# Second channel product by one level of Strassen's method, token groups of 512, and a new order

## The chip, the cores and the metric

The kernel runs on one core of one Trainium2 chip. The metric is the device time of one execution in microseconds (us), a median of runs. The engines are PE (matmul), with its weight loads PEld beside it, DVE (vector), ACT (scalar), POOL (GpSimd) and SP, which issues the DMAs. Each engine works its own queue in order; a semaphore wait at the head of a queue holds all that stands behind it.

## The reference, cut to what matters

Three layers in a row, on 2 samples x 768 tokens x 384 channels, all in fp32:

```python
y[t]  = rt @ (state + u * outer(kt, vt))           # layer 1: attention, per head of 48,
state = wt[..., None] * state + outer(kt, vt)      #          over 768 steps
h = gelu(x @ w_in); u, v = h[..., :512], h[..., 512:]
x = x + (u * (w_sg @ (norm(v) * g) + b_sg)) @ w_out        # layer 2: gated MLP
u  = x + (relu(x.T @ w_tok1) @ w_tok2).T           # layer 3: mixer, 768 -> 256 -> 768
return u + relu(u @ w_ch1) @ w_ch2                 #          and 384 -> 1536 -> 384
```

## The kernel before, in words

Every fp32 operand of a large product is held as two parts, hi (a copy rounded to the matmul's fp32r type) and lo (the rest). `prod` makes a product from three matmuls into one PSUM tile: hi.hi (L257), hi.lo (L258), lo.hi (L259).

The weights arrive as 64-bit floats and are converted on the chip in chunks, in three stages (`advance`): stage 0 two ACT instructions (L214, L215), stage 1 two on DVE (L217, L219), stage 2 a hi copy on ACT (L224) and the lo subtraction on POOL (L226; on DVE for the early weights). A chunk waits in one of four buffers named st; a freed buffer is loaded again by a DMA that SP issues.

The order of all work before the channel stage is written by hand in two strings, ORDER (attention and the first product of layer 2) and LAST (the rest of layer 2, token products, staging). Each letter calls one part: 0, 1, 2 advance one chunk by that stage; w is one keep-warm matmul (L125); P and Y are the attention's outputs (L608; L617 and L623), Q its state sum (L641, L647), i and j the first token product and its eviction (T1p, T1e), k and l the second (T2p, T2e), m one C1 of token group 0. p frees the transposed inputs and opens the last pools. L617 and L647 add a vector that DVE has made, or the old state, into the PSUM sum, by a matmul with the identity.

The mixer's channel stage works on four groups of 384 tokens. `C1(h, j)` makes hidden tile j (of 12) of group h: nine matmuls of 384 columns, then `relu_split`: ACT writes hi (L398), DVE lo (L399). `C2(h, j, ct)` adds hidden tile j into the output tile ct (of 3): three matmuls of 384. The first C1 group stands in LAST (m); `rest()` then alternates C1(h+1, j) and the three C2(h, j, ct), and at the end C2 of group 3, one ct after the other, each with one DVE add (L454) and one store (L455).

PSUM has eight banks; in the channel stage five turn for C1 and three hold the sums of C2.

## Time and profile before

| | us |
|---|---|
| median of 3 runs (lowest, highest) | 390.64 (390.48, 390.92) |
| the profiled execution | 391.98 |
| its span, first to last instruction | 390.3 |
| PE busy | 379.9 (97%) |
| DVE busy | 233.5 (60%) |
| ACT busy | 187.8 (48%) |
| POOL busy | 133.1 (34%) |

The rows that follow below come from this profiled execution. A row of the time line gives the start of an instruction, its duration, engine, line, operation, the tile written and those read, and a count; matmuls overlap, so what one costs is the distance from its start to the next one's. In brackets stands the idle time ahead, with its releaser.

### The profile page before, as it was taken

How to read it: one execution, taken by the hardware profiler on the slowest of the kernel's cores; microseconds unless marked ns; L12 is line 12 of the kernel's file. 1: busy time of each engine (PE TensorE's matmuls, PEld its weight loads, DVE VectorE, ACT ScalarE, POOL GpSimd, SP SyncE). 2: the span in 40 equal slices, each digit the busy share in tenths (PEclk: the TensorE clock that was granted, in tenths of full speed). 3: DMA queues.
4: the chain of work that ended last, by engine and by line, in shares of the span. 5: the costliest groups of instructions: out<-in, count | busy, mean ns of one | idle time of the engine just before them, and what ended most of it. 6: DMA issues, size and time to landing. Idle time of an engine off the chain costs nothing.

```text
span 390.3 us, 7950 instructions
## 1 busy us (share of the span) xinstructions
PE 379.9 (97%) x3229; PEld 354.8 (91%) x3229; DVE 233.5 (60%) x396; ACT 187.8 (48%) x427; POOL 133.1 (34%) x149
## 2 busy tenths in 40 slices
PE   8899999999999999999999999999999999999994
PEld 3487788889999799999999999999999999999993
DVE  7999998889797575794486674782133114211320
ACT  3699878887345795754546674741111111111000
POOL 2325577763543356567544651350000000000000
PEclk9999999999999999999999999999999999999998
DMA  7575375453361014322433242400010001000110
GB/s 238 172 215 181 100 246 155 122 156 114 94 214 42 2 40 123 107 66 71 123 102 102 81 126 78 121 3 0 3 44 18 1 0 62 0 2 0 64 40 27
DMA packets 15581, 33.68 MB, mean 86 GB/s; under 512 B 2352, under 2 KB 5680, under 8 KB 15536
## 3 DMA queue, kind: packets, MB, share of 16 engines
q1 hardware_dynamic: 15536, 33.09, 27.9%
q8 instruction: 27, 0.44, 0.5%
q14 instruction: 18, 0.15, 0.1%
HBM read 30.72 MB, written 2.36 MB: 85 GB/s over the span
## 4 chain that ended last, share of the span: by engine, by line
PE 83%; POOL 4%; ACT 3%; issue 3%; DVE 3%; DMA 2%; SPq 1%; POOLq 0%; ACTq 0%
PE mm L257 23%; PE mm L258 23%; PE mm L259 23%; PE py L623 3%; PE pa L582 2%; PE py L608 2%; DMA st<-in_dram 1%; PE tr L282 1%; POOL vs L367 1%; PE pkv L641 1%; DMA kr<-in_dram 1%; PE mm L567 1%; PE mm L420 1%; PE py L617 1%; PE pt L595 1%
## 5 line engine op out<-in xcount | busy, mean ns | idle before, releaser
L399 DVE SCALAR_TENSOR_TENSOR cl<-mm,ch 128x384 fp32r<-128x384 f32 x48 | 26.5, 556 | 83.9 <-ACT ch L398 83.9
L398 ACT ACTIVATE ch<-mm 128x384 fp32r<-128x384 f32 x48 | 23.4, 492 | 93.1 <-PE mm L259 93.0
L217 DVE SCALAR_TENSOR_TENSOR st<-st 128x384 int32<-128x384 int32 (+1 forms) x50 | 30.3, 607 | 9.5 <-ACT st L215 7.9
L219 DVE SCALAR_TENSOR_TENSOR st<-st 128x384 int32<-128x384 int32 (+1 forms) x50 | 33.2, 665 | 1.7
L214 ACT ACTIVATE st<-st 128x384 f32<-128x384 f32 (+1 forms) x50 | 25.8, 517 | 9.3 <-DMA st<-in_dram 9.3
L588 POOL TENSOR_SCALAR_AFFINE_SELECT A<-A 128x512 f32<-128x512 f32 x24 | 18.3, 770 | 33.5 <-ACT A L587 32.0
L215 ACT ACTIVATE st<-st 128x384 int32<-128x384 uint32 (+1 forms) x50 | 25.5, 510 | 0.0
L369 ACT ACTIVATE gh<-vs 128x384 fp32r<-128x384 f32 x16 | 8.4, 524 | 32.9 <-POOL vs L367 32.9
L367 POOL TENSOR_TENSOR vs<-vs,uT 128x384 f32<-128x384 f32 x16 | 19.2, 1205 | 11.6 <-DVE vs L365 11.6
L560 POOL TENSOR_TENSOR rk<-kr 112x512 f32<-112x512 f32 x12 | 19.0, 1580 | 11.4 <-DMA kr<-in_dram 11.4
L257 PE MATMUL mm<-xt,wuh 128*128 128x256 f32 x72 | 20.8, 289 | 0.0
L259 PE MATMUL mm<-xt,wul 128*128 128x256 f32 x72 | 20.3, 282 | 0.0
L258 PE MATMUL mm<-xt,wuh 128*128 128x256 f32 x72 | 20.3, 282 | 0.0
L534 DVE TENSOR_TENSOR_SCAN wf<-wf,scan 112x516 f32<-112x516 f32 x12 | 19.0, 1583 | 1.6 <-DMA wf<-in_dram 1.6
L548 DVE TENSOR_TENSOR_SCAN wf<-wf,scan 112x516 f32<-112x516 f32 x12 | 17.8, 1480 | 0.4
L391 POOL TENSOR_TENSOR x1l<-x,x1h 128x384 fp32r<-128x384 f32 x12 | 14.0, 1173 | 10.4 <-ACT x1h L390 10.4
L125 PE MATMUL mm<-scan 112*128 112x512 bf16 x49 | 14.2, 431 | 3.1 <-DVE scan L673 1.7
L556 DVE TENSOR_TENSOR kr<-kr,wf 112x1024 f32<-112x1024 f32 x12 | 15.9, 1328 | 1.2 <-DVE wf L548 0.2
L257 PE MATMUL mm<-ch,c20h 128*128 128x384 f32 x48 | 16.1, 336 | 0.2 <-DVE o L454 0.2
L257 PE MATMUL mm<-woh,gh 128*128 128x384 f32 x48 | 16.2, 338 | 0.0
L259 PE MATMUL mm<-woh,gl 128*128 128x384 f32 x48 | 16.1, 336 | 0.0
L257 PE MATMUL mm<-uh,c10h 128*128 128x384 f32 x48 | 16.1, 336 | 0.0
(188 smaller groups left out, 1233.3 us busy)
## 6 DMA issues: line engine op xcount, KB each, us to landing
st<-in_dram SPq DMA_DIRECT2D x38, 384.0 KB, 3.4
kr<-in_dram SPq DMA_DIRECT2D x12, 448.0 KB, 4.3
st<-in_dram SPq DMA_DIRECT2D x18, 256.0 KB, 4.2
...
ub<-in_dram SPq DMA_DIRECT2D x1, 3.5 KB, 4.6
```

The costliest lines, as they stand in the source:

```text
L214: nc.scalar.activation(high.bitcast(F32), high.bitcast(F32), AF.Copy, scale=REBIAS)
L215: nc.scalar.activation(low, low.bitcast(U32), AF.Copy, scale=TOP3, bias=FLOOR)
L217: nc.vector.scalar_tensor_tensor(low, high, -2 ** 31, low, op0=ALU.bitwise_and, op1=ALU.bitwise_or)
L219: nc.vector.scalar_tensor_tensor(low, high, 3, low, op0=ALU.logical_shift_left, op1=ALU.bitwise_or)
L257: mm(out, w[0], x[0], start=first, stop=False, skip_group_check=True)
L258: mm(out, w[0], x[1], start=False, stop=False, skip_group_check=True)
L259: mm(out, w[1], x[0], start=False, stop=last, skip_group_check=True)
L367: nc.gpsimd.tensor_tensor(t, t, self.uT[d, h], op=ALU.mult)
L398: nc.scalar.activation(hi, ps, AF.Relu)
L399: nc.vector.scalar_tensor_tensor(lo, ps, 0.0, hi.bitcast(F32), op0=ALU.max, op1=ALU.subtract)
L534: nc.vector.tensor_tensor_scan(WF[i][:, WCOL + 2:], WF[i][:, :NHP * CW], scan1.rearrange("p h c -> p (h c)"), 0.0, op0=ALU.mult, op1=ALU.add)
L560: nc.gpsimd.tensor_tensor(RK[i][:PR], KR[i][:, 0], KR[i][:, 1], op=ALU.mult)
```

## The change

The channel stage now takes three groups of 512 tokens. C1(g, k) makes hidden tiles 2k and 2k+1, each by nine matmuls of 512 columns. For the pair of hidden tiles (b1, b2), each split in two halves of 256 tokens, and the first two output tiles, C2(g, k) forms the 2 x 2 block product by seven block products of 256 columns instead of eight (Winograd's form of Strassen's method), three matmuls each; the third output tile is done directly by four (C2d). So a step has 33 matmuls of 256 in C2 and 18 of 512 in C1, and there are 18 steps.

The method needs sums on both sides. Sums of weight blocks are made once, on POOL (`sums_of_weights`) and ACT with POOL (`split_sums`), for k = 0 before the first step and for each next k beside it. Sums of activations (ta, tb) are made in the eviction of C1, which is now eight DVE and six ACT instructions a step. At the end of a group `finish` combines the seven products with the residual (which POOL makes in steps 1 to 3 of each group) in eight DVE adds, one ACT copy and three POOL adds, `finish_rest` in two more DVE adds, and six stores of 256 tokens go out. Of the last group, 24 direct matmuls of k = 4 and 5 stand after the last Strassen product.

T2 follows the groups: its parts are 512, 256, 256, 512 tokens wide per output tile (EDGES). The identity matmuls L617 and L647 are issued in two column halves, 64 wide. C1 no longer stands in LAST. Both strings are new; keep-warm matmuls are 49 as before. Pools moved, and C1 turns three PSUM banks, C2 five.

```diff
@@ -25,6 +25,9 @@
 EPS = 1e-6
 NHP = H // 2
 PR = 112
+G = 2 * P
+EDGES = 0, 4, 6, 8, 12
+BPAD = 112
@@ -55,14 +58,14 @@
 ORDER = (
-    "w0010w 1www1w w201Tw wwtwqL FSQwUw wZwAge ww0wwo Kw0Nw1 20F2ww ww1qw2 2wTYyt SoXxe2 PUQA0Z KgVYL0 qyS1XN T10eAF "
+    "w00q10 T11t2w ww0QZg 10wwww wU0FwS wANwwK wwwqwe wNowww Lw1202 T1Y22F StUAyX PoxQ2Z eKg0V0 LY11Sy qXeT0N AoFUB0 "
...
 LAST = (
...
-    "2mij1j 0mlmkk k01lkk 1k22l0 l20ll0 11210m 1222l")
+    "01122i 0lkjjk klk200 11l2k1 kl01ll 2kll22")
...
@@ -407,7 +411,7 @@
             self.prod(ps, self.wp("t1", k, c, DTOK), self.x1[b * NC + k], k == 0, k == NC - 1)
     def T1e(self, n):
-        hi, lo = self.a2(F32R, E, "hh"), self.a2(F32R, E, "hl")
+        hi, lo = self.a15(F32R, "hh"), self.a15(F32R, "hl")
         self.relu_split(self.tps.pop(n), hi, lo)
         self.tok[n] = hi, lo
@@ -415,44 +419,154 @@
         nc, (h, ct) = self.nc, divmod(n, 3)
         c = slice(ct * P, (ct + 1) * P)
-        ps = self.ups[n] = self.mm(E)
-        for j in range(3):
-            nc.tensor.matmul(ps[:, j * P:(j + 1) * P], self.x[3 * h + j][:, c], self.ident,
-                             is_transpose=True, start=(j == 0), stop=False, skip_group_check=True)
+        n0, n1 = EDGES[h:h + 2]
+        ps = self.ups[n] = self.mm((n1 - n0) * P)
+        for j in range(n0, n1):
+            nc.tensor.matmul(ps[:, (j - n0) * P:(j - n0 + 1) * P], self.x[j][:, c], self.ident,
+                             is_transpose=True, start=(j == n0), stop=False, skip_group_check=True)
         for j in range(2):
             self.prod(ps, [t[:, c] for t in self.tok[h // 2 * 2 + j]],
-                      self.wp("t2", j, slice(h % 2 * E, (h % 2 + 1) * E), S), False, j == 1)
+                      self.wp("t2", j, slice((n0 - h // 2 * NC) * P, (n1 - h // 2 * NC) * P), S), False, j == 1)
     def T2e(self, n):
-        nc, ps = self.nc, self.ups.pop(n)
-        hi, lo = self.a15(F32R, "uh"), self.a15(F32R, "ul")
+        nc, ps, (h, ct) = self.nc, self.ups.pop(n), divmod(n, 3)
+        g, at = divmod(EDGES[h], 4)
+        if at == 0:
+            self.u[g, ct] = self.a2(F32R, nm="uh"), self.a2(F32R, nm="ul")
+        hi, lo = (t[:, at * P:(at + EDGES[h + 1] - EDGES[h]) * P] for t in self.u[g, ct])
         nc.scalar.activation(hi, ps, AF.Copy)
         nc.vector.tensor_tensor(lo, ps, hi.bitcast(F32), op=ALU.subtract)
-        self.u[divmod(n, 3)] = (hi, lo)
-    def C1(self, h, j):
...
-    def C2(self, h, j, ct):
...
+    def big(self, nm, pool=None, dt=F32R):
+        return (pool or self.pbig).tile([P, 2 * G], dt, tag="big", name=self.nm(nm))
+    def sums_of_weights(self, k):
+        nc, i, b = self.nc, k // 2, k % 2 * 2
+        if k == 0:
+            self.ws = []
+        if k % 3 == 0:
+            self.ws.append([self.pw.tile([P, 3 * 512], F32R, tag="w", name=self.nm("s" + q)) for q in "hl"])
+        hi, lo = (t.rearrange("p (k c) -> p k c", c=E)[:, b:b + 2, :2 * P].bitcast(F32) for t in self.w[f"c2{i}"])
+        f = self.pst.tile([P, S], F32, tag="st", name=self.nm("f"))[:, :512]
+        self.sw = t = self.pst.tile([P, S], F32, tag="st", name=self.nm("sw"))[:, :512]
+        add = nc.gpsimd.tensor_tensor
+        add(f.rearrange("p (k c) -> p k c", k=2), hi, lo, op=ALU.add)
+        a11, a21, a12 = (f[:, q * P:(q + 1) * P] for q in range(3))
+        a22 = f[:, 3 * P:]
+        s1, s2, s3, s4 = (t[:, q * P:(q + 1) * P] for q in range(4))
+        add(s1, a21, a22, op=ALU.add)
+        add(s2, s1, a11, op=ALU.subtract)
+        add(s3, a21, a11, op=ALU.subtract)
+        add(s4, a12, s2, op=ALU.subtract)
+    def split_sums(self, k):
+        hi, lo = (t[:, k % 3 * 512:(k % 3 + 1) * 512] for t in self.ws[k // 3])
+        self.nc.scalar.activation(hi, self.sw, AF.Copy)
+        self.nc.gpsimd.tensor_tensor(lo, self.sw, hi.bitcast(F32), op=ALU.subtract)
+    def C1(self, g, k):
+        nc, ps = self.nc, []
+        for j in (2 * k, 2 * k + 1):
+            p = self.mm(2 * G)
+            c = slice(j * P, (j + 1) * P)
+            for q in range(3):
+                self.prod(p, self.wp(f"c1{q}", 0, c, DCH), self.u[g, q], q == 0, q == 2)
+            ps.append(p)
+        p1, p2 = ps
+        one, two = slice(0, G), slice(G, 2 * G)
+        sub = lambda o, x, y: nc.vector.scalar_tensor_tensor(o, x, 0.0, y, op0=ALU.max, op1=ALU.subtract)
+        act = nc.scalar.activation
+        r, ta, tb = (self.big(q, self.ptmp, F32) for q in ("r", "ta", "tb"))
+        h1, l1 = self.big("h1"), self.big("l1")
+        act(r[:, one], p1[:, one], AF.Relu)
+        act(h1, p1, AF.Relu)
+        sub(ta[:, one], p1[:, two], r[:, one])
+        sub(l1, p1, h1.bitcast(F32))
+        h2, l2 = self.big("h2"), self.big("l2")
+        act(r[:, two], p2[:, two], AF.Relu)
+        act(h2, p2, AF.Relu)
+        sub(ta[:, two], p1[:, two], r[:, two])
+        nc.vector.tensor_tensor(tb[:, one], r[:, two], ta[:, one], op=ALU.subtract)
+        sub(tb[:, two], p2[:, one], tb[:, one])
+        sub(l2, p2, h2.bitcast(F32))
+        self.hid[g, k] = [(h1, l1), (h2, l2)]
+        for t in (ta, tb):
+            hi, lo = self.big("th"), self.big("tl")
+            act(hi, t, AF.Copy)
+            nc.vector.tensor_tensor(lo, t, hi.bitcast(F32), op=ALU.subtract)
+            self.hid[g, k].append((hi, lo))
+    def C2w(self, k, b, ct):
+        j = 2 * k + b
+        return self.wp(f"c2{j // 4}", j % 4, slice(ct * P, (ct + 1) * P), E)
+    def C2(self, g, k):
+        if k == 0:
+            self.acc = [self.mm(2 * G, self.ps5) for _ in range(5)]
+        one, two = slice(0, G), slice(G, 2 * G)
+        b1, b2, ta, tb = self.hid[g, k]
+        w = lambda q: [t[:, k % 3 * 512 + q * P:k % 3 * 512 + (q + 1) * P] for t in self.ws[k // 3]]
+        a = self.acc
+        m = {1: (a[0], one, self.C2w(k, 0, 0), b1, one), 2: (a[2], one, self.C2w(k, 1, 0), b2, one),
+             3: (a[2], two, w(3), b2, two), 4: (a[3], one, self.C2w(k, 1, 1), tb, two),
+             5: (a[1], one, w(0), ta, one), 6: (a[0], two, w(1), tb, one), 7: (a[1], two, w(2), ta, two)}
+        end = (g, k) == (B * S // (2 * G) - 1, DCH // G - 1)
+        for q in (1, 2, 3, 6, 7, 5, 4) if end else (1, 2, 3):
+            self.C2m(k, *m[q], q in (1, 2, 4, 7) if end else q in (1, 2))
+        if not end:
+            if (g, k) not in self.later:
+                self.C2d(g, k)
+            for q in (5, 7, 6, 4):
+                self.C2m(k, *m[q], q in (5, 4))
+    def C2m(self, k, acc, o, w, x, c, start):
+        self.prod(acc[:, o], w, [t[:, c] for t in x], start and k == 0, k == DCH // G - 1)
+    def C2d(self, g, k, halves=(0, 1)):
+        for t in halves:
+            c = slice(t * G, (t + 1) * G)
+            for b in range(2):
+                self.prod(self.acc[4][:, c], self.C2w(k, b, 2), [x[:, c] for x in self.hid[g, k][b]],
+                          k == 0 and t == 0 and b == 0, k == DCH // G - 1 and b == 1)
+    def residual(self, g, ct):
+        hi, lo = self.u[g, ct]
+        o = self.oo[:, 2 * ct * G:(2 * ct + 2) * G]
+        self.nc.gpsimd.tensor_tensor(o, hi.bitcast(F32), lo.bitcast(F32), op=ALU.add)
+    def store(self, g, ct, t):
+        self.nc.sync.dma_start(self.out[ct * P:(ct + 1) * P, (2 * g + t) * G:(2 * g + t + 1) * G], self.o[ct, t])
+    def finish(self, g):
+        nc, a, o = self.nc, self.acc, self.o
+        s1, s2, s3, s4 = self.part
+        one, two = slice(0, G), slice(G, 2 * G)
+        add = lambda to, x, y: nc.vector.tensor_tensor(to, x, y, op=ALU.add)
+        more = lambda to, x: nc.gpsimd.tensor_tensor(to, to, x, op=ALU.add)
+        nc.scalar.activation(s1, a[0][:, one], AF.Copy)
+        more(o[0, 0], s1)
+        add(o[0, 0], a[2][:, one], o[0, 0])
+        self.store(g, 0, 0)
+        add(o[0, 1], a[2][:, two], o[0, 1])
+        add(s2, a[0][:, two], s1)
+        add(s3, a[1][:, two], s2)
+        add(s4, a[1][:, one], s2)
+        more(o[1, 0], s3)
+        add(o[1, 1], a[1][:, one], o[1, 1])
+        add(o[0, 1], o[0, 1], s4)
+        self.store(g, 0, 1)
+        more(o[1, 1], s3)
+        self.store(g, 1, 1)
+        add(o[1, 0], a[3][:, one], o[1, 0])
+        self.store(g, 1, 0)
+    def finish_rest(self, g, t):
+        self.nc.vector.tensor_tensor(self.o[2, t], self.acc[4][:, t * G:(t + 1) * G], self.o[2, t], op=ALU.add)
+        self.store(g, 2, t)
@@ -483,21 +597,49 @@
     def rest(self, sound=None, flag=None, look=None):
         okc = sound() if sound else None
...
+        self.top.close()
+        self.pbig = self.ctx.enter_context(self.tc.tile_pool(name="big", bufs=24, reuse_waits="tile"))
+        self.pbig.tile([P, BPAD], F32, name="bpad", bufs=1)
+        self.ptmp = self.ctx.enter_context(self.tc.tile_pool(name="tmp", bufs=3, reuse_waits="tile"))
+        self.banks = [self.ps3]
+        n, last = DCH // G, B * S // (2 * G) - 1
+        steps = [(g, k) for g in range(last + 1) for k in range(n)]
+        self.later = [(last, k) for k in range(n - 3, n)]
+        self.sums_of_weights(0)
+        self.C1(0, 0)
+        self.split_sums(0)
+        for i, (g, k) in enumerate(steps):
+            if i < n - 1:
+                self.sums_of_weights(i + 1)
+            if i + 1 < len(steps):
+                self.C1(*steps[i + 1])
+            if i < n - 1:
+                self.split_sums(i + 1)
+            if i == 0:
+                o, part = (self.pw.tile([P, 6 * G], F32, tag="w", name=self.nm("o")) for _ in range(2))
+                self.oo = o
+                self.o = {(ct, t): o[:, (2 * ct + t) * G:(2 * ct + t + 1) * G] for ct in range(3) for t in range(2)}
+                self.part = [part[:, q * G:(q + 1) * G] for q in range(4)]
+            if sound and i == 1:
+                flag(okc)
+            if look and i == len(steps) - 2:
                 look()
+            if 1 <= k <= 3:
+                self.residual(g, k - 1)
+            if i + 1 == len(steps):
+                self.C2d(*self.later[0])
+            self.C2(g, k)
+            if k == n - 1 and g < last:
+                self.finish(g)
+                for t in range(2):
+                    self.finish_rest(g, t)
+        for t in range(2):
+            for x in self.later[1:]:
+                self.C2d(*x, (t,))
+        self.finish(last)
+        for t in range(2):
+            self.finish_rest(last, t)
...
@@ -614,8 +756,9 @@
                 if i % NC == 0:
                     PY[i] = psa.tile([P, E], F32, tag="y", name=f"py{i}")
                 if i < ADDED:
-                    nc.tensor.matmul(PY[i], dn.ident, AV[i], start=(i % NC == 0), stop=False,
-                                     skip_group_check=True)
+                    for t in HALF:
+                        nc.tensor.matmul(PY[i][t], dn.ident[:, t], AV[i], start=(i % NC == 0), stop=False,
+                                         skip_group_check=True)
@@ -644,8 +787,9 @@
                                          start=(hp == 0), stop=(i % NC == 0 or i >= ADDED),
                                          skip_group_check=True)
                 if i % NC and i < ADDED:
-                    nc.tensor.matmul(pkv, dn.ident[:PR, :PR], SC[1 - i % 2], start=False, stop=True,
-                                     skip_group_check=True)
+                    for q in (slice(0, 64), slice(64, PR)):
+                        nc.tensor.matmul(pkv[q], dn.ident[:PR, q], SC[1 - i % 2], start=False, stop=True,
+                                         skip_group_check=True)
                 KV[i] = pkv
@@ -733,7 +877,7 @@
-                i=dn.T1p, j=dn.T1e, k=dn.T2p, l=dn.T2e, m=lambda j: dn.C1(0, j))
+                i=dn.T1p, j=dn.T1e, k=dn.T2p, l=dn.T2e)
```

Three places show how instructions moved. First PE in before, where the channel stage begins: the end of the first C1 of group 1, and the C2 behind it. uh, ul are the token product's output, c10 to c12 and c20 to c22 the weights of the two channel products; in before ch, cl is the hidden tile, in after h, l are the hidden tiles and sh, sl the sums of weights; lines 261 to 263 in after are 257 to 259 in before.

```order
L257 MATMUL mm_3524<-uh_3358,c12h_2911 128x384
L258 MATMUL mm_3524<-ul_3359,c12h_2911 128x384
L259 MATMUL mm_3524<-uh_3358,c12l_2912 128x384
L257 MATMUL mm_3538<-ch_3058,c20h_3156 128x384
L258 MATMUL mm_3538<-cl_3059,c20h_3156 128x384
L259 MATMUL mm_3538<-ch_3058,c20l_3157 128x384
L257 MATMUL mm_3544<-ch_3058,c20h_3156 128x384
```

And PE in after, at the second C1 and the first C2:

```order
L261 MATMUL mm_3442<-uh_3158,c12h_2842 128x512
L262 MATMUL mm_3442<-ul_3159,c12h_2842 128x512
L263 MATMUL mm_3442<-uh_3158,c12l_2843 128x512
L261 MATMUL mm_3481<-h_527_3401,c20h_2990 128x256
L262 MATMUL mm_3481<-l_528_3402,c20h_2990 128x256
L263 MATMUL mm_3481<-h_527_3401,c20l_2991 128x256
L261 MATMUL mm_3483<-h_529_3407,c20h_2990 128x256
L262 MATMUL mm_3483<-l_530_3408,c20h_2990 128x256
L263 MATMUL mm_3483<-h_529_3407,c20l_2991 128x256
L261 MATMUL mm_3483<-h_529_3407,sh_3369 128x256
L262 MATMUL mm_3483<-l_530_3408,sh_3369 128x256
L263 MATMUL mm_3483<-h_529_3407,sl_3370 128x256
```

The third product of the new step, the seventh matmul behind C1, is the first that reads a sum of weights (sh, sl).

Second POOL in before at the same time, from the last staged chunks (c22l) on. f is hi + lo of a weight pair, sw the four sums, sl their lo part; the next row of before is a register load at the end of the program.

```order
L226 TENSOR_TENSOR c22l_3485<-st_3297,c22h_3484 128x384
L226 TENSOR_TENSOR c22l_3485<-st_3448,c22h_3484 128x384
L226 TENSOR_TENSOR c22l_3485<-st_3452,c22h_3484 128x384
L226 TENSOR_TENSOR c22l_3485<-st_3466,c22h_3484 128x384
L767 TENSOR_LOAD fi
```

And POOL in after, from the same chunks on:

```order
L230 TENSOR_TENSOR c22l_3291<-st_3110,c22h_3290 128x384
L230 TENSOR_TENSOR c22l_3291<-st_3197,c22h_3290 128x384
L230 TENSOR_TENSOR c22l_3291<-st_3201,c22h_3290 128x384
L230 TENSOR_TENSOR c22l_3291<-st_3278,c22h_3290 128x384
L454 TENSOR_TENSOR f_3371<-c20h_2990,c20l_2991 128x512
L458 TENSOR_TENSOR sw_3372<-f_3371 128x128
L459 TENSOR_TENSOR sw_3372<-sw_3372,f_3371 128x128
L460 TENSOR_TENSOR sw_3372<-f_3371 128x128
L461 TENSOR_TENSOR sw_3372<-f_3371,sw_3372 128x128
L466 TENSOR_TENSOR sl_3370<-sw_3372,sh_3369 128x512
L454 TENSOR_TENSOR f_3425<-c20h_2990,c20l_2991 128x512
```

The sums of the first step stand behind the staging of the last weights, though they read only c20.

Third PE in before at the first attention output without a state: pt are transposes, py the output, pa the next scores; av is the vector added by the identity.

```order
L595 MATMUL pt_354<-ident,kr_140 128x112 x4
L617 MATMUL py_359<-av_279,ident 128x384
L623 MATMUL py_359<-vn_132,A_282 64x48 x8
L623 MATMUL py_359<-vn_132,A_295 64x48 x8
L582 MATMUL pa_1_381<-kr_140 64x128 x2
```

And PE in after, at the same output:

```order
L737 MATMUL pt_334<-ident,kr_140 128x112 x4
L760 MATMUL py_341<-av_272,ident 64x384 x2
L766 MATMUL py_341<-vn_132,A_300 64x48 x8
L766 MATMUL py_341<-vn_132,A_307 64x48 x8
L724 MATMUL pa_1_370<-kr_140 64x128 x2
```

One matmul of 128 output columns has become two of 64, at the same place.

## Rows read from the trace of the kernel before

**Rows 1.** The page: busy time by engine, and the chain of waits by engine.

```profile
PE 379.9 (97%) x3229; PEld 354.8 (91%) x3229; DVE 233.5 (60%) x396; ACT 187.8 (48%) x427; POOL 133.1 (34%) x149
...
PE 83%; POOL 4%; ACT 3%; issue 3%; DVE 3%; DMA 2%; SPq 1%; POOLq 0%; ACTq 0%
```

**Rows 2.** Table by stretch: PE, PEld, DVE, ACT, POOL busy, clock, DMA share, GB/s.

```profile
260.00:380.00 120.00, 119.83 (x692) 119.26 (x691) 31.77 (x64) 17.24 (x36) 0.48 (x1) 1.00 0.05 17
```

**Rows 3.** Waits of PE: line, releaser, us in total, times, longest.

```profile
PE mm L257 <- DVE xt L291: 0.9, 1, 0.9
PE mm L258 <- POOL t2l L226: 0.5, 1, 0.5
PE mm L257 <- DVE o L454: 0.2, 1, 0.2
```

**Rows 4.** Time line of PE, two stretches of matmuls of 256 columns, first and last.

```profile
61.62 0.36 PE L257 MATMUL mm<-xt,wuh 128*128 128x256 f32 x1
...
63.73 0.28 PE L259 MATMUL mm<-xt,wul 128*128 128x256 f32 x1
...
147.78 0.28 PE L259 MATMUL mm<-xt,wul 128*128 128x256 f32 x1
...
151.49 0.34 PE L257 MATMUL mm<-woh,gh 128*128 128x384 f32 x1
```

**Rows 5.** Time line of PE, nine matmuls of 256 columns, then nine of 512.

```profile
136.19 0.28 PE L257 MATMUL mm<-xt,wuh 128*128 128x256 f32 x1
...
137.25 0.40 PE L257 MATMUL mm<-wvh,xt 128*128 128x512 f32 x1
...
139.32 0.28 PE L257 MATMUL mm<-xt,wuh 128*128 128x256 f32 x1
```

**Rows 6.** Time line of PE at two attention outputs (64-wide and 128-wide identity products).

```profile
18.78 0.82 PE L617 MATMUL py<-av,ident 128*128 128x384 f32 x2
19.53 0.38 PE L623 MATMUL py<-vn,A 128*64 128x48 f32 x6
...
30.15 0.88 PE L608 MATMUL py<-state,kr 112*64 112x96 f32 x16
30.96 0.91 PE L617 MATMUL py<-av,ident 128*128 128x384 f32 x2
31.80 1.14 PE L623 MATMUL py<-vn,A 128*64 128x48 f32 x32
```

**Rows 7.** Groups by line: duration in ns, min/median/max, first and last start.

```profile
L399 DVE SCALAR_TENSOR_TENSOR cl<-mm,ch x48: 546/557/560, 215.5 to 364.6; 128x384 fp32r<-128x384 f32 x48
...
L325 DVE TENSOR_TENSOR vl<-v,vh x12: 657/690/1035, 37.8 to 161.9; 128x512 fp32r<-128x512 f32 x12
...
L560 POOL TENSOR_TENSOR rk<-kr x12: 1262/1457/2260, 5.3 to 115.2; 112x512 f32<-112x512 f32 x12
...
L226 POOL TENSOR_TENSOR t1l<-st,t1h x6: 748/842/1112, 166.9 to 187.5; 128x256 fp32r<-128x256 f32 x6
...
L302 ACT ACTIVATE v<-mm x12: 573/587/600, 27.2 to 147.0; 128x512 f32<-128x512 f32 x12
```

**Rows 8.** Time line: PE at C1(1,0), POOL at the last staged chunk.

```profile
252.75 0.33 PE L257 MATMUL mm<-uh,c10h 128*128 128x384 f32 x1
...
259.45 1.03 POOL L226 TENSOR_TENSOR c22l<-st,c22h 128x384 fp32r<-128x384 f32 x1 [1.08 <-ACT c22h L224]
```

**Rows 9.** Time line of POOL and DVE: the same scan beside POOL and alone.

```profile
5.26 1.26 POOL L560 TENSOR_TENSOR rk<-kr 112x512 f32<-112x512 f32 x1 [3.05 <-DMA kr<-in_dram]
5.29 2.31 DVE L548 TENSOR_TENSOR_SCAN wf<-wf,scan 112x516 f32<-112x516 f32 x1
...
15.72 1.23 DVE L548 TENSOR_TENSOR_SCAN wf<-wf,scan 112x516 f32<-112x516 f32 x1
```

**Rows 10.** Time line of the end: the last matmul, the last store's issue.

```profile
384.40 0.34 PE L259 MATMUL mm<-ch,c22l 128*128 128x384 f32 x1
...
385.36 0.33 SPq L455 DMA_DIRECT2D out_dram<-o  x1
```

51 lines of the change are left out of this document (8 added, 43 removed), and 4 rows, old and new, of the table ORDER.

## The prediction

> **What bounds the kernel now.** Read the page's first part first: PE is busy 97% of the span and no other computing engine above 60% [rows 1] (weight loads, at 91%, run beside the matmuls). The chain of waits then says that this busy time is also the path: PE holds 83% of it, nobody else more than 4% [rows 1]. Then the table by stretch: from 260 to 380 us, the channel stage alone, PE is busy 119.83 of 120 us at a granted clock of 1.00 (2.4 GHz), with 692 matmuls [rows 2]. So there a matmul of 384 columns costs 120/692 = 173.4 ns, and DVE (31.77) and ACT (17.24) have room. The waits of PE are few: apart from keep-warm matmuls at the start only 0.9, 0.5 and 0.2 us in the whole program [rows 3]. The time is therefore the sum of what PE issues, plus stalls that are new, plus the tail. What the other engines do counts only where PE comes to wait for it.
>
> **The unit prices.** 31 matmuls of 256 columns start from 147.78 up to the next kind at 151.49: 3.71/31 = 119.7 ns each [rows 4]. Nine of 512 columns run from 137.25 to 139.32: 230 ns each [rows 5]. Both are rows of PE at full clock, each matmul with a weight load of its own, as in the new code. (A straight line through the two has 0.431 ns a column and 9.4 ns a matmul; the 384 columns measured lie 1.5 ns below it.)
>
> **The change, part by part, on PE.**
>
> Second channel product. Before: 4 groups x 12 hidden tiles x 3 channel tiles x 3 = 432 matmuls of 384, 432 x 173.4 = 74.9 us. After: 18 steps x 33 (seven Strassen products and four direct ones, three matmuls each) = 594 of 256, 594 x 119.7 = 71.1. That is -3.8. Other stretches of the same matmul give the bounds: 117.8 (nine from 136.19 to 137.25 [rows 5]) and 124 (17 spacings from 61.62 to 63.73 [rows 4]), so -4.9 to -1.2.
>
> First channel product. 432 x 173.4 = 74.9 becomes 324 of 512, 324 x 230 = 74.5: -0.4; the same relative spread, -1.6% to +3.6%, gives -1.6 to +2.3.
>
> Token product: 72 x 173.4 = 12.5 becomes 36 x 230 + 36 x 119.7 = 12.6: +0.1. The three together: -4.1, from -6.4 to +1.2. The work saved on paper (an eighth of two thirds of the second product, 6.2 us) is larger than that, because shorter matmuls cost more per column.
>
> Column halves of the identity products. L617 (7 times) and L647 (4 times) become pairs of 64 columns, each with the same two records of 384 or 192 elements. L608 shows that halves run beside each other: 16 half-wide records of 96 elements take 0.81 us (30.15 to 30.96), 53 ns each; the two full-wide records of 384 at L617 take 0.75 us after a 128-wide neighbour (18.78 to 19.53) and 0.84 after a 64-wide one (30.96 to 31.80) [rows 6]. So a pair costs what one cost (halves at L608's pace would be 8 x 2 x 53 = 0.85), and a change of width, 0.09 us, goes at one or both ends: I take 0.1 for each of the 11, -1.1. Bounds: -2.2 (two changes each) to +6.8, if the two halves ran one after the other: 7 x 0.75 for L617, and half as much, for half the columns, 4 times for L647.
>
> Keep-warm matmuls: 49 in both, only moved. They fill time in which PE would wait anyway; +/-0.5 for the new places.
>
> **Stalls.** The three of [rows 3], 1.6 us, sit at places that the new order rearranges; I take them as gone, bounds 0 and -1.6. Two new ones. (a) T2p of the second sample follows closer on T1e of its hidden tiles: at most one DVE eviction of 0.56 [rows 7], take 0.3. (b) The important one: the third Strassen product of step 0 reads the sums of weights. On POOL they stand behind the last c22l (order of POOL, above), and on PE they are wanted after two C1 (36 x 230 = 8.3 us) and six matmuls (0.7): 9.0 us after the first C1 starts. On POOL a pass takes: two of 512 elements at 1.26 (the shortest of L560 [rows 7]), four of 128 at about half of that for 256 (0.75 is the shortest of t1l), 0.4 each, and ACT's copy at 0.59 [rows 7]: 2.5 + 1.6 + 0.6 = 4.7, with the usual L560 median of 1.46, 5.1. In the trace of before the last c22l ends at 259.45 + 1.03 = 260.48, while C1(1,0), the first product behind the string, starts at 252.75 [rows 8]: 7.7 us late. With that lateness sums are there 12.8 us after C1 starts and PE waits 3.8. But in the new string the twelve C1 with their evictions (12 x 0.56 on DVE [rows 7], and as many on ACT) no longer stand between the staging steps, so these engines get to them sooner; with only the copy and the subtraction behind (2 us) there is no wait. Bounds 0 and 3.8; I take 1.2. Behind a PE that waits there is queued everything else; evictions of C1(0,1) are done by then and lose nothing. In steps 1 to 5 the sums have a whole step of 18 x 230 + 33 x 119.7 = 8.1 us for 5.1 us of POOL and its share of residuals (1.5).
>
> DVE and ACT in a steady step: DVE takes 0.56 for 384 elements (L399) and 0.69 for 512 (L325), so some 0.43 for 256 by the same slope: 4 x 0.43 + 4 x 0.69 = 4.5 us; ACT at most 6 x 0.59 = 3.5 [rows 7]. Both lie under PE's 8.1. One row speaks against this. The scan L548 took 2.31 us where a POOL product L560 began 0.03 before it, and 1.23 where POOL was still [rows 9]: DVE was held until POOL's instruction ended. The Trainium skill (page "SBUF — State Buffer", section "SBUF: two separate sides") says that a DVE operation with two SBUF inputs and a GpSimd operation that reads SBUF exclude each other for whole instructions; the trace agrees (2.31 = 1.23 + nearly all of 1.26). Only three of the eight DVE operations of a step have two SBUF inputs, so in steps 0 to 5 DVE needs at most 4.5 + 3 x 1.3 = 8.4: even so it barely passes PE's 8.1, and three PSUM banks let it lag. No cost taken; if the cover went, 0.2 x 6 = 1.2.
>
> Group ends. finish() is ten DVE adds, one ACT copy and three POOL adds, in the middle of the program beside C1 of the next group's second step (4.1 us) and not waited for by PE before the next C2 needs bank 0: ten at 0.43 = 4.3 and three POOL at 0.75. Cost 0 to 0.5 twice, take 0.2 in all.
>
> Tail. Before: the last matmul starts at 384.40, behind it comes one add of 384 on DVE, the store issues at 385.36, and the span of 390.3 ends 4.9 us later [rows 10]. After: 24 direct matmuls, 24 x 119.7 = 2.9 us, stand behind the last Strassen product, beside eight DVE adds (3.4 us, with POOL between) and before two more of 0.43. DVE finishes about 0.5 later than one add of 384 would; the last stores are smaller. +0.4, bounds -0.2 and +2.
>
> **The sum**, against the profiled execution of 391.98 (span 390.3): products -4.1, halves -1.1, old stalls -1.6, new ones +0.3 +1.2 +0.2, tail +0.4: -4.7, that is 387.3 there. The median of the runs shown is 390.64, 1.3 below the profiled one; the same -4.7 gives 385.9.
>
> **Rivals.**
>
> Staging as late as before (0.25). The sums come 3.8 us late instead of 1.2: 388.5, still faster. For it: ACT and DVE were held by staging up to 260 in before [rows 8]. If the string brings the last c22l later still, each us adds one: from 5.9 us of waiting on the kernel is slower than before.
>
> Halves one after the other (0.05). +6.8 in place of -1.1 gives 393.8, slower. It decides from the point where a pair costs more than 0.4 us above the one that it replaces (11 x 0.43 = 4.7). Against it: L608's 53 ns for 96 elements, where L617's full-wide records take 375 ns for 384, 94 for 96 [rows 6].
>
> Fixed price of a matmul (0.03). The change issues 990 matmuls for 936 and 345,600 columns for 359,424. If the 13,824 columns saved (0.431 ns each, 6.0 us) were outweighed by 54 more starts, a start would have to cost 110 ns; the rows give 9.4. With 256 columns at, say, 135 ns, if weight loads came through ([rows 4] show 119.7), C2 would take 594 x 135 = 80.2 and the kernel 395. The Trainium skill (page "TensorE: Matmul & The Clock Gate", section "Back-to-back issue gap") gives a sustained price that falls per column as matmuls grow (81 ns at 128, 131 at 512); interpolated, an estimate, 256 would be 98 and 384 114, C2 +9 and C1 -7. The trace contradicts both levels (119.7 and 173.4 [rows 2, 4]).
>
> Nothing new waits (0.17). Old stalls go, no new ones, the lower pace of 117.8: 385.9 - 1.7 - 1.1 = 383.1.
>
> My forecast has 0.43: 384.3 to 387.5 by itself. The remaining 0.07 is a mishap of the new order before the channel stage, such as a DMA landing late at a new place in the first 130 us: +2 to +5, 388 to 391.
>
> **Range and chances.** 382.4 to 390.2 leaves the halves in series, the fixed price and the worst of the staging and the mishaps out above (0.13), and some 0.06 below. Within 0.2%, 0.78 us, which is about what a measurement of this kernel can tell from no change, is 389.86 to 391.42: parts of the late staging and the mishaps, 0.07. Slower: halves 0.05, price 0.03, and 0.03 of the others, 0.11. Faster: 0.82.
>
> **What would show it.** Steady steps of the new channel stage with PE busy over 99%, 256-column spacing near 120 and 512-column near 230 ns; C1 plus C2 over 18 steps in 146 us. The pair at the new L760 starting its next neighbour 0.75 to 0.85 us later. One wait of PE on sl of about 1 us at the first third product, none at later steps. DVE ending within 1.5 us of the last matmul. It is wrong if the spacing of 256 columns in C2 is over 126 ns, if PE waits for POOL in each of the first six steps, or if PE waits for st or sl longer than 5 us.

## The result, and the profile after

The changed kernel takes 394.65 us (median; its executions lie between 391.42 and 396.89), the kernel before 390.98 on the same chips. The ratio is 1.0083, with an interval of 1.0062 to 1.0104: slower, where 385.9 and faster was forecast. The profiled execution went from 391.98 to 396.09, +4.1 us. Ratios and intervals here and below leave out one execution, the 397.68 of E2, which lies more than 1.5% above the fastest of its kernel.

The page after, to be held against [rows 1]: busy time, the clock row of 40 slices, and the chain of waits by engine.

```profile
PE 377.2 (96%) x3305; PEld 335.6 (85%) x3305; DVE 287.3 (73%) x498; ACT 224.5 (57%) x496; POOL 183.2 (46%) x203
...
PEclk9789999999999999999999999999999999999996
...
PE 46%; POOL 22%; issue 11%; DVE 9%; ACT 7%; DMA 3%; SPq 0%; POOLq 0%; DVEq 0%; ACTq 0%
```

PE is busy 2.7 us less, yet the span is 4.0 longer, and the chain, 83% PE before, is now 46% PE. Two slices of the clock row, 10 to 30 us, are below full. So PE has less to do and spends more of the span not doing it, or doing it slowly.

The channel stage first. The table by stretch (columns as in [rows 2]) and three rows of PE's time line, the start of a step, of its C2 and of the next step:

```profile
262.00:374.00 112.00, 112.00 (x712) 101.86 (x711) 66.39 (x132) 44.54 (x90) 31.94 (x34) 1.00 0.04 15
```

```profile
301.36 0.39 PE L261 MATMUL mm<-uh,c10h 128*128 128x512 f32 x1
...
305.44 0.28 PE L261 MATMUL mm<-h,c20h 128*128 128x256 f32 x1
...
309.33 0.39 PE L261 MATMUL mm<-uh,c10h 128*128 128x512 f32 x1
```

C1 takes 4.08 us (18 at 226.7 ns), C2 3.89 (33 at 117.9), a step 7.97 against the 8.1 of the prediction, and PE never waits in it, though DVE's share has gone from 26% to 59%. This part did what it should and a little more. The time is lost in front of it and behind it. The waits of PE after ([rows 3] has those of before):

```profile
PE mm L129 <- DVE av L715: 1.7, 1, 1.7
PE mm L129 <- DVE scan L817: 1.7, 1, 1.7
PE mm L263 <- POOL sl L466: 0.8, 1, 0.8
PE pa L724 <- issue: 0.8, 1, 0.8
PE pa L724 <- ACT A L729: 0.7, 1, 0.7
PE mm L262 <- DVE sg2l L230: 0.6, 1, 0.6
PE pt L737 <- DVE kr L698: 0.5, 1, 0.5
PE mm L261 <- ACT sg2h L228: 0.3, 1, 0.3
PE pa L724 <- DVE kr L698: 0.2, 1, 0.2
```

The three waits of [rows 3] are gone in this trace; one on sl is at the place foreseen; six others, 3.1 us, stand in the attention and the gate (pa, pt, sg2), where before had none. And the wait on av at the start is followed by a stretch at half speed, first in PE's time line of after, then in the table by stretch:

```profile
13.17 0.61 PE L129 MATMUL mm<-scan 112*128 112x512 bf16 x2
15.52 1.87 PE L129 MATMUL mm<-scan 112*128 112x512 bf16 x4 [1.74 <-DVE av L715]
...
21.68 1.15 PE L760 MATMUL py<-av,ident 128*64 128x384 f32 x4
```

```profile
12.00:15.00 3.00, 1.77 (x35) 1.07 (x35) 2.91 (x5) 2.96 (x8) 1.30 (x1) 1.00 0.91 300
15.00:22.00 7.00, 6.48 (x32) 3.20 (x33) 6.81 (x11) 3.36 (x10) 4.93 (x3) 0.53 0.49 149
```

The kernel before at the same place, PE's time line and the same two stretches:

```profile
12.69 1.47 PE L125 MATMUL mm<-scan 112*128 112x512 bf16 x6
15.57 1.89 PE L125 MATMUL mm<-scan 112*128 112x512 bf16 x8 [1.41 <-DVE av L573]
```

```profile
12.00:15.00 3.00, 2.16 (x30) 1.13 (x23) 2.93 (x5) 0.00 (x0) 1.28 (x1) 1.00 0.63 227
15.00:22.00 7.00, 6.36 (x98) 4.11 (x98) 6.78 (x12) 6.81 (x18) 1.89 (x2) 1.00 0.53 153
```

PE stood idle for 1.74 us up to 15.52, and from 15 to 22 us the granted clock is 0.53, nearly all of it at the lower level, 1.2 GHz; keep-warm matmuls then take 0.43 us each. In before PE waited 1.41 us for the same vector, with six keep-warm matmuls ahead of the wait where after has two, and the clock stayed at full. The traces of E2 and E6 below, which have the ORDER of after, show the fall again (0.55 and 0.76 in these 7 us, behind waits of 1.8 and 1.5 us). The first attention output (L617, now L760) starts at 21.68 where it started at 18.78 [rows 6].

The end, PE's last matmul, DVE's last adds and the last store's issue, to be held against [rows 10]:

```profile
384.80 0.28 PE L263 MATMUL mm<-h,c22l 128*128 128x256 f32 x1
```

```profile
385.62 0.74 DVE L568 TENSOR_TENSOR o<-mm,o 128x256 f32<-128x256 f32 x2
```

```profile
387.83 2.06 SPq L541 DMA_DIRECT2D out_dram<-o  x1
```

DVE's last add in before:

```profile
384.77 0.56 DVE L454 TENSOR_TENSOR o<-mm,o 128x384 f32<-128x384 f32 x1 [5.22 <-PE mm L259]
```

Behind the last matmul's start DVE needs 1.6 us (before 0.9), but SP is at its last issue until 389.89, and the span ends 9.5 us behind that matmul, where it was 5.9.

Where the 4.1 us come from, by the distances between the starts of PE's matmuls, summed by kind over both traces:

| | before | after | |
|---|---|---|---|
| first and second channel product (with the wait on sl, 1.0) | 150.25 | 144.47 | -5.8 |
| second token product (before: with the wait on t2l) | 14.41 | 13.63 | -0.8 |
| identity products, state sum ahead of L647 | 9.84 | 9.19 | -0.65 |
| all else up to the channel stage | 208.25 | 215.85 | +7.6 |
| last matmul's start to the end of the span | 5.9 | 9.5 | +3.6 |

### The profile page after: what moved, and what is told of

The parts are those of the page before. It is cut to its first block, busy times and chain, and to the rows that moved or that the text cites. A ratio compares the mean times of both kernels' runs of the same rounds, so it can differ in the third digit from the quotient of the medians.

```text
span 394.3 us, 8407 instructions
## 1 busy us (share of the span) xinstructions
PE 377.2 (96%) x3305; PEld 335.6 (85%) x3305; DVE 287.3 (73%) x498; ACT 224.5 (57%) x496; POOL 183.2 (46%) x203
## 4 chain that ended last, share of the span: by engine, by line
PE 46%; POOL 22%; issue 11%; DVE 9%; ACT 7%; DMA 3%; SPq 0%; POOLq 0%; DVEq 0%; ACTq 0%
PE mm L261 13%; PE mm L263 13%; PE mm L262 13%; POOL vs L371 3%; DMA kr<-in_dram 2%; POOL x1l L395 2%; POOL rs L318 2%; POOL rk L702 2%; DVE st L221 2%; POOL A L730 2%; PE py L766 1%; PE pa L724 1%; POOL wol L230 1%; PE mm L129 1%; DVE wf L676 1%
## 5 line engine op out<-in xcount | busy, mean ns | idle before, releaser
L479 DVE SCALAR_TENSOR_TENSOR ta<-mm,r 128x256 f32<-128x256 f32 x36 | 15.2, 422 | 47.0 <-ACT h L484 40.2
L549 POOL TENSOR_TENSOR o<-o,o 128x256 f32<-128x256 f32 x9 | 7.0, 796 | 80.0 <-ACT o L550 74.8
L223 DVE SCALAR_TENSOR_TENSOR st<-st 128x384 int32<-128x384 int32 (+1 forms) x50 | 40.7, 814 | 1.7
L730 POOL TENSOR_SCALAR_AFFINE_SELECT A<-A 128x512 f32<-128x512 f32 x24 | 20.6, 870 | 39.6 <-ACT A L729 39.6
L221 DVE SCALAR_TENSOR_TENSOR st<-st 128x384 int32<-128x384 int32 (+1 forms) x50 | 30.0, 599 | 7.1 <-ACT st L219 4.3
L218 ACT ACTIVATE st<-st 128x384 f32<-128x384 f32 (+1 forms) x50 | 25.7, 515 | 15.4 <-DMA st<-in_dram 15.3
L483 ACT ACTIVATE r<-mm 128x256 f32<-128x256 f32 x18 | 6.9, 384 | 44.4 <-PE mm L263 44.4
L479 DVE SCALAR_TENSOR_TENSOR l<-mm,h 128x512 fp32r<-128x512 f32 x36 | 24.5, 680 | 0.0
L129 PE MATMUL mm<-scan 112*128 112x512 bf16 x49 | 16.5, 474 | 3.4 <-DVE av L715 1.7
L729 ACT ACTIVATE A<-pa 128x512 f32<-128x512 f32 x24 | 13.6, 593 | 7.7 <-PE pa L724 7.7
L488 ACT ACTIVATE r<-mm 128x256 f32<-128x256 f32 x18 | 6.9, 384 | 18.5 <-PE mm L263 18.5
L676 DVE TENSOR_TENSOR_SCAN wf<-wf,scan 112x516 f32<-112x516 f32 x12 | 15.7, 1311 | 1.6 <-DMA wf<-in_dram 1.6
L329 DVE TENSOR_TENSOR vl<-v,vh 128x512 fp32r<-128x512 f32 x12 | 8.3, 690 | 10.8 <-ACT vh L328 10.6
```

The lines of the kernel that those rows point to most:

```text
L129: nc.tensor.matmul(ps, noise[:, :P], noise, start=True, stop=True)
L218: nc.scalar.activation(high.bitcast(F32), high.bitcast(F32), AF.Copy, scale=REBIAS)
L221: nc.vector.scalar_tensor_tensor(low, high, -2 ** 31, low, op0=ALU.bitwise_and, op1=ALU.bitwise_or)
L223: nc.vector.scalar_tensor_tensor(low, high, 3, low, op0=ALU.logical_shift_left, op1=ALU.bitwise_or)
L479: sub = lambda o, x, y: nc.vector.scalar_tensor_tensor(o, x, 0.0, y, op0=ALU.max, op1=ALU.subtract)
L730: nc.gpsimd.affine_select(out=t, in_=t, pattern=[[0, NHP], [1, P]], compare_op=ALU.is_gt, fill=0.0, base=0, channel_multiplier=-1)
```

## The experiments

Theory: the products gain what was forecast; the gain went to the new order of the front (one fall of the clock, and a handful of waits) and to the tail (six stores and the sums ahead of them, crowded at the end). Rivals: the Strassen form costs PE time itself; the pools or the halves slow the front; the tail is what any store's landing takes. Medians and ratios are against the kernel before in the same series (391.1 for E1 to E4, 391.1 for E5 to E8, 390.7 for E9 to E11). The series ran on different chips, and the kernel before differs by up to 0.4 us between them; so differences of a few tenths between runs of two series say nothing.

**E1, the idle stretch filled.** In ORDER one keep-warm matmul ahead of it becomes eight:

```diff
- ... wU0FwS wANwwK ...
+ ... wU0FwS wAN*wK ...
...
+            parts["*"] = lambda: dn.keep_warm(8, noise)
```

> The changed kernel with seven more keep-warm matmuls in one place of ORDER, ahead of the idle stretch of PE from about 13.8 to 15.5 us (0.215 us each, so 1.5 us of it). Theory 1 (the granted clock falls to 1.2 GHz because PE is idle there, and stays low from 15.3 to 22.2 us): the clock row stays at full, the first attention output starts near 18.7 instead of 21.7 us, the kernel is about 3 us faster than the changed kernel in its disturbed executions, 391.5 to 392.5 in the median (1.001 to 1.004 of the kernel before), and the spread of 391.4 to 396.9 shrinks to under 2 us. Rival (the loss is the sum of waits that the new order makes, the clock follows from them): no change, 394 to 395.

392.17 us (390.26 to 394.09), 1.0029 (1.0009 to 1.0048): 2.5 less than the changed kernel, the lowest of the executions 1.2 less, the spread 3.8 instead of 5.5. The table by stretch:

```profile
12.00:15.00 3.00, 3.00 (x42) 1.66 (x41) 2.94 (x3) 2.95 (x8) 1.33 (x1) 1.00 0.95 307
15.00:22.00 7.00, 6.86 (x102) 4.15 (x100) 6.78 (x11) 4.21 (x12) 5.10 (x3) 1.00 0.51 154
```

The clock stays at full and the first output starts at 19.09, 2.6 us earlier. Not all of it arrives: PE now meets a wait of 1.0 us on DVE (xt) at 25.61, which the slow stretch had covered, and the wait on sl is not there in this trace. The first C1 starts at 238.80, only 1.4 us earlier than in after. The theory holds for the clock: it is at full in this stretch, and in all twelve executions its mean over the whole execution is 0.992 or more. The gain is a little smaller than expected, since PE meets the wait on DVE there; and the spread was to shrink to under 2 us, which it did not.

**E2 and E3, stores of the last group from SP and ACT in turn**, without and with E1's edit:

```diff
+        q = self.nc.scalar if g == B * S // (2 * G) - 1 and (ct + t) % 2 else self.nc.sync
-        self.nc.sync.dma_start(self.out[ct * P:(ct + 1) * P, (2 * g + t) * G:(2 * g + t + 1) * G], self.o[ct, t])
+        q.dma_start(self.out[ct * P:(ct + 1) * P, (2 * g + t) * G:(2 * g + t + 1) * G], self.o[ct, t])
```

> The changed kernel with the six stores of the last group issued alternately by SP and by ACT, which is idle then. Theory 1 (the six issues stand one behind the other on SP: the last begins at 387.83, 1.5 us after its data is there, and takes 2.06 us): the end of the span moves from 9.5 us behind the last matmul's start to 6.5 to 7.5, the kernel 2 to 3 us faster than the changed kernel, 392 to 392.5. Rival (the tail is the DVE and POOL sums and the landing of the last store, not its issue): under 0.5 us, 394 to 395.

> Both edits, seven keep-warm matmuls in the idle stretch and stores from two queues. Theory 1: the two gains add, 5 to 6 us off the changed kernel's 394.65, 389 to 390, that is 0.995 to 0.998 of the kernel before: faster than it. Rival (one bound stands behind both): not below 391.

E2: 393.28 (391.02 to 397.68), 1.0044 (1.0027 to 1.0060). E3: 392.33 (390.36 to 392.99), 1.0023 (1.0010 to 1.0036), no better than E1 in what the intervals can tell. The end of E3, the last matmul, SP's three stores and the last two of ACT's three:

```profile
382.46 0.28 PE L263 MATMUL mm<-h,c22l 128*128 128x256 f32 x1
```

```profile
380.70 3.90 SPq L542 DMA_DIRECT2D out_dram<-o  x3
```

```profile
383.86 0.86 ACTq L542 DMA_DIRECT2D out_dram<-o  x2
```

In E3 the last issue of the two queues is done 2.3 us behind the last matmul, where it was 5.1 in E1, yet the span ends 8.5 us behind it, 1.2 less than in E1 (9.7) and only 0.3 less than in E4 and E5 (8.8), which issue all from SP. The stores' last data packets end 5.9 us behind the last matmul in E3, 6.1 in E1 and after, 5.7 in E5. So the queue of issues on SP is at most a small part of the 3.6 us: with five of the six stores handed out behind the last matmul, the data land late however they are issued. Expected 2 to 3 us: a miss. E2's median is 1.4 under the changed kernel's, but where the clock did not fall (mean 0.992 or more) E2 takes 392.8 and the changed kernel 392.9: no gain of the stores shows there, and E2 had fewer falls (4 of 12, the changed kernel 10 of 19; see E11 for this sign).

**E4, the two strings of before** (without its C1) in the changed kernel.

> The changed kernel with the two strings of the kernel before (without their twelve C1). Channel stage, halves and tail stay those of the changed kernel. Theory 1: everything ahead of the channel stage costs what it did before, so the first C1 starts 4 to 6 us earlier than the 240.2 of the changed kernel, unless the staging then comes late; tail still +3.5; 389 to 391 in all. Rival (the pools and the halves slow the front, not the order): 394 to 396. A third way: without the C1 between, the last c22l is late and PE waits 3 to 6 us for the sums at the first third product: 393 to 395, with the wait shown on sl.

402.95 (402.38 to 403.34), 1.0299 (1.0284 to 1.0315). The two longest waits of PE:

```profile
PE mm L261 <- DVE ta L479: 4.7, 1, 4.7
PE mm L262 <- POOL x1l L395: 3.2, 3, 2.0
```

Neither of the first two: the front is good (the last attention transpose at 129.06, 1.35 earlier than in before), but the old LAST without the C1 that stood in it runs dry. PE waits for POOL (x1l) in the token product, and for 4.7 us in the second C1 for a PSUM bank of the first, which DVE, still at the staging of the last weights, has not evicted. Behind these waits the granted clock is 0.50 (225 to 230 us) and 0.56 (250 to 255 us), which makes them dearer; the listed waits between 200 and 256 us come to 9.4 us. The third way was expected on sl; it came on ta, of the same cause. A new LAST was needed.

**E5, ORDER of before, LAST of after** (less the seven letters that the old ORDER has done).

> The changed kernel with ORDER of the kernel before and its own LAST, less the first V, B, M, N, b, c and d, which ORDER of before has issued already. E4 showed that this front, with the halves, has the clock at full and reaches the last attention output near 129 us, and that the old LAST without C1 lets PE wait 15 us between 220 and 260. Theory 1 (the new ORDER costs some 5 to 6 us, through one fall of the clock and a dozen waits of PE, and the new LAST is needed for the staging): first C1 at 234 to 236 instead of 240.2, 388 to 390 in the median, 0.993 to 0.998 of the kernel before. Rival (the two strings fit only together, so that waits come back in LAST): 392 or more, with waits of PE between 130 and 240.

389.66 (388.83 to 391.32), 0.9968 (0.9955 to 0.9981): 5.0 us less than the changed kernel and faster than before. All waits of PE:

```profile
PE mm L261 <- ACT uT L345: 2.1, 3, 1.4
PE mm L129 <- DVE scan L817: 1.7, 1, 1.7
PE mm L261 <- DVE xt L295: 0.9, 1, 0.9
PE mm L129 <- DVE av L715: 0.5, 1, 0.5
PE py L766 <- POOL A L730: 0.2, 1, 0.2
```

The first C1 starts at 234.96 instead of 240.20, with the clock at full throughout the front. The six waits in attention and gate are gone, but for 0.2 on a score tile (A); at the seam of the two strings, 155 to 160 us, PE waits 1.9 us for ACT. So the new ORDER cost 5 us. Half of it goes with the fall of the clock (E1: 2.5). Where the other half went, the lists of waits do not show: without those of keep-warm matmuls they come to 3.2 us here and to 3.3 in E1. By the distances between matmul starts the front is 3.8 us shorter than in E1, 2.7 of it at the keep-warm matmuls and PE's waits in front of them (49 of them, 56 in E1).

**E6, the second channel product direct**: per step 18 matmuls of 512 columns, no sums, one add and one store for each output tile.

```diff
...
-            self.acc = [self.mm(2 * G, self.ps5) for _ in range(5)]
...
+            self.acc = [self.mm(2 * G, self.ps5) for _ in range(3)]
+        for ct in range(3):
             for b in range(2):
...
+                self.prod(self.acc[ct], self.C2w(k, b, ct), self.hid[g, k][b], k == 0 and b == 0,
+                          k == DCH // G - 1 and b == 1)
...
```

> The changed kernel with the second channel product direct: per step 18 matmuls of 512 columns in place of 33 of 256, no sums of weights or activations, output tile after output tile with one DVE add and one store of 256 KB each. By the rows of the changed kernel a step of 33 takes 3.88 us and 18 of 512 take 4.08: +3.6 us on PE. The tail: last add 0.7, one store to issue, so 5.5 to 6.5 us behind the last matmul instead of 9.5, -3 to -4. Theory 1 (what Strassen saves on PE is given back in the tail): 394 to 395.5, no difference from the changed kernel. Rival (sums and evictions of the Strassen form also cost PE time in the steps): 391 to 393.

395.64 (395.34 to 396.08), 1.0115 (1.0100 to 1.0129), 1.0 above the changed kernel, less than the two's spread. By matmul starts the direct product takes 75.5 us, the Strassen form 69.8 (E1): 5.7 saved on PE, not 3.6. The tail:

```profile
388.08 0.40 PE L263 MATMUL mm<-h,c22l 128*128 128x512 f32 x1
```

```profile
389.30 0.33 SPq L498 DMA_DIRECT2D out_dram<-o  x1
```

The span ends at 394.4, 6.3 us behind the last matmul instead of 9.5. So 3.2 of the 5.7 go back in the tail. That is the way the theory went, but it had all of the gain go back, and 2.5 are left. The medians show only 1.0 of it. But the changed kernel's median holds executions with the long fall of the clock, and E6's four (mean clock 0.994 or more) do not; against the changed kernel's executions without it (392.9, see E11) E6 is 2.7 slower. The rival (Strassen costs PE time in its steps) is out.

**E7, the kernel before with only the column halves** (the two hunks of L617 and L647).

> The kernel before with only the column halves of the two identity products. By the account of PE's stream, the halves and their neighbours take 1.4 us less in the changed kernel, at full clock. Theory 1: 1.0 to 1.4 us faster than the kernel before, 0.9965 to 0.9975, the last attention output 1.3 us earlier. Rival (PE waits at that place for DVE anyway): no change, 0.999 to 1.001.

390.26 (389.92 to 391.44), 0.9991 (0.9979 to 1.0002): not to be told from no change, and less than the 1.0 to 1.4 us expected. Its time line of PE at the outputs of [rows 6]:

```profile
17.82 0.87 PE L618 MATMUL py<-av,ident 128*64 128x384 f32 x4
18.52 0.39 PE L624 MATMUL py<-vn,A 128*64 128x48 f32 x8
...
29.85 0.82 PE L618 MATMUL py<-av,ident 128*64 128x384 f32 x4
30.50 0.62 PE L624 MATMUL py<-vn,A 128*64 128x48 f32 x16
```

A pair takes 0.70 and 0.65 us, one product took 0.75 and 0.84: the two halves run beside each other. Over both lines and the state sum ahead of L647 PE's stream is 0.6 shorter. All of it is at L617 (5.40 to 4.82 us in seven places): the four pairs of L647 take 1.90 where four single products took 1.40, and the state sums ahead of them 0.5 less.

**E8 and E11, fewer keep-warm matmuls in the kernel before**, at its idle stretch: four left out (E8, the first four of those below), then ten (E11, whose edit this is).

```diff
- ... FSQwUw wZwAge ww0wwo Kw0Nw1 ...
+ ... FSQU ZAge 0o K0N1 ...
```

> The kernel before with four of its keep-warm matmuls left out, those right ahead of PE's idle stretch (12.7 to 13.5 us), so that PE is idle for some 2.2 us there instead of 1.4. Theory 1 (the clock falls when this stretch is longer, and stays low for about 7 us): the clock row shows 0.5 behind it, the kernel is 1.5 to 3 us slower than before, and its times spread by several us. Rival (idle time there does not decide the clock): no change, clock at full.

E8: 391.36 (390.39 to 393.06), 1.0007 (0.9994 to 1.0020). It did not do what it was meant to: four of the later ones moved up, PE was busy for 2.80 of the 3 us up to 15 and its wait on av was 1.0 us, shorter than in before. The clock stayed at full; the case that it was to make did not come about.

> The kernel before with ten of its keep-warm matmuls left out around PE's idle stretch. In E8, with four left out, later ones had moved up, PE was idle no longer than before (1.0 us) and the clock stayed full. Here none are left to move up, so PE is idle for 2 us or more between 13 and 17 us. Theory 1 (the length of this stretch decides): the clock row falls to 0.5 between 15 and 18 us for 3 to 7 us, and the median is 1 to 3 us above the kernel before, with a wider spread. Rival (the fall comes from something else in the changed kernel): clock at full, no change within 0.2%.

E11: 392.34 (390.45 to 396.07), 1.0046 (1.0018 to 1.0073). The two idle stretches in PE's time line, and the table by stretch:

```profile
14.74 0.63 PE L567 MATMUL mm<-ub,rk 112*64 112x2 f32 x16 [1.09 <-POOL rk L560]
...
17.29 1.01 PE L595 MATMUL pt<-ident,kr 112*128 112x112 f32 x4 [1.00 <-DVE kr L556]
```

```profile
12.00:15.00 3.00, 1.91 (x33) 1.11 (x30) 2.88 (x8) 0.85 (x3) 1.55 (x1) 1.00 0.72 253
15.00:22.00 7.00, 6.00 (x66) 3.95 (x66) 6.78 (x12) 5.74 (x16) 1.90 (x2) 0.53 0.58 168
```

With the fillers away the kernel before has the fall too, at the same place and to the same 0.53. So it does not need anything else of the changed kernel. But the idle time came in two pieces, 1.09 and 1.00 us, and the clock was low from 15.4 us on, before the second; each is shorter than the 1.41 us of before, behind which the clock stayed at full. So the length of one idle stretch, on which the expectation rested, is not what decides; what does, these runs do not show.

Only the profiled executions have a trace; of the others the mean granted clock is known. In six of E11's twelve executions it is 0.991 or more (their median 391.8), in six 0.987 or less (393.9). Of the changed kernel's nineteen, ten have 0.988 or less and a median of 395.7, nine 0.992 or more and 392.9: taken by this sign, which marks the long falls alone (E6's trace has a shorter one at a mean of 0.994), the fall does not come each time, which is a part of its spread. The rest is of another cause: each of the two groups spreads by over 3 us, as E1 does without it.

**E9 and E10, another end of the last group**, on E1 and on E5. Strassen for the last group's first five steps; finish() then runs beside the sixth step, which is direct, and beside all direct matmuls of the third tile from k = 3 on:

```diff
...
+        self.finish(last)
+        for ct in range(2):
+            p = self.mm(2 * G)
+            for b in range(2):
+                self.prod(p, self.C2w(n - 1, b, ct), self.hid[last, n - 1][b], b == 0, b == 1)
+            o = self.oo[:, 2 * ct * G:(2 * ct + 2) * G]
+            self.nc.vector.tensor_tensor(o, p, o, op=ALU.add)
+            self.nc.sync.dma_start(self.out[ct * P:(ct + 1) * P, 2 * last * G:(2 * last + 2) * G], o)
         for t in range(2):
-            for x in self.later[1:]:
+            for x in self.later:
                 self.C2d(*x, (t,))
-        self.finish(last)
...
```

> E1 (the changed kernel with its idle stretch filled) with another end of the last group: Strassen for its first five steps only, the sixth direct. finish() of the five steps then runs beside 12 direct matmuls of 512 and 36 of 256 (2.8 and 4.2 us), two output tiles leave 4.2 us before the last matmul in stores of 256 KB, and only two stores of 128 KB are left. PE +0.3 us. Theory 1 (the tail is six stores and the sums ahead of them, crowded behind the last Strassen product): the span ends 6 to 6.8 us behind the last matmul instead of 9.7, so 388.7 to 389.7 against E1's 392.2. Rival (the tail is the landing of any store): 8.5 us or more behind it, 391.5 or more.

> E5 (ORDER of the kernel before, own LAST) with the same new end of the last group. If front and tail are the two places where the gain of the products went, both gains add: 386 to 387, 0.988 to 0.990 of the kernel before. Rival: the tail gives nothing here, 389.5.

E9: 389.53 (388.95 to 390.72), 0.9964 (0.9950 to 0.9979), 2.6 under E1. E10: 386.63 (386.51 to 388.57), 0.9886 (0.9866 to 0.9907), 3.0 under E5 and 4.1 under the kernel before: the fastest of all. The tail of E10, the last matmul, then SP's stores:

```profile
380.74 0.28 PE L263 MATMUL mm<-h,c22l 128*128 128x256 f32 x1
```

```profile
378.20 0.93 SPq L655 DMA_DIRECT2D out_dram<-o  x2
381.51 0.81 SPq L553 DMA_DIRECT2D out_dram<-o  x2
```

Two stores of 256 KB leave before the last matmul, two of 128 KB behind it, and the span ends 6.1 us behind it (E9: 6.1; before: 5.9). The profiled execution of E10 is the slowest of its six, with a wait of 2.0 us on xt that E5's trace does not have.

## Why the prediction was wrong, point by point

Unit prices and products: right in mechanism, and the gain was larger. 256 columns took 117.9 ns (119.7 forecast), 512 took 226.7 (230), a step 7.97 (8.1); the two products gave -5.8 with the wait on sl in them (1.0 by matmul starts), against -4.2 and +1.2; in E1's trace, which has no such wait, they gave -6.9, a little beyond the bounds (-4.9 and -1.6, together -6.5). The fixed price of a matmul as a rival is out: it needed some 135 ns for 256 columns. The Trainium skill (page "TensorE: Matmul & The Clock Gate", section "Back-to-back issue gap") puts a sustained matmul of 512 columns at 131 ns; the rows here show 226.7.

The sums of weights: right in place and size. PE waited 0.84 us for sl at the first third product in the profiled execution, 0 in E1's, never at a later step. The last c22l ended 4.3 us behind the start of the first C1, between the bounds of 7.7 and 2.

DVE and POOL in the steps, group ends: right. DVE rose to 0.59 of the stretch and PE waited for neither.

Halves: right in mechanism, the size too large: -0.6 measured in PE's stream, -1.1 forecast. In time E7 leaves it open between -0.8 and +0.1 us. The 0.1 that was taken for each of the eleven came at the seven of L617 alone.

Tail: wrong. "+0.4, bounds -0.2 and +2" counted the adds on DVE, which did end only 0.6 later than in before, and took the stores for free because "the last stores are smaller". Measured +3.6. Before, two of the last three stores had left with the first two output tiles; now five of six are issued behind the last matmul's start. Their data land later with that: the last data packet ends 3.5 us behind the last matmul in before, 6.1 in after and 2.7 in E10. A second queue (E3) gives back 0.3 to 1.2 of it in the traces and nothing in time that could be told; handing out two thirds of the data earlier (E9, E10) gives back 2.7 to 3.6 in the traces (E5 8.8 to 6.1, E1 9.7 to 6.1) and 2.6 to 3.0 in time.

The front: wrong, and the larger part. The step was "Keep-warm matmuls: 49 in both, only moved. They fill time in which PE would wait anyway; +/-0.5 for the new places", with "I take them as gone" on the old stalls. The old stalls did go in the profiled execution (-1.6), but the one on xt is back where the clock is at full (1.0 in E1, 0.9 in E5). And the order of the attention was new as a whole, and I priced only two of its waits. It brought 3.1 us of others, and it left PE idle for 1.74 us behind two fillers where six had stood; there the clock fell, which cost 2.6 us at the first output and 2.5 in the median (E1; E11 has the fall in the kernel before). These two come to 5.7 of the +7.6 that the table shows for the front; the rest stands in no wait of the lists and is not explained. E5 puts the price of the new ORDER at 5.0. The case that came nearest was the mishap of the new order, +2 to +5, to which 0.07 was given, and it needed the tail with it.

With another front and another end the change gives about what was forecast, -4.1 in E10 against -4.7. That is not the sum come true term by term: in E10's trace the two products give -6.8, all that stands ahead of them +3.1 and the tail +0.2. What is still open: which single moves of the new ORDER make the six waits, and why the fall comes in some executions and not in others. The wait on av itself moves between executions of one order (1.41 us in before, none in E7, whose edit lies behind it); DMA landings would do that, but no run shows it.
